# Left-over query units moved to the end of the loop in an attention, expert and router kernel

## The chip, the cores and the metric

The kernel runs on one core of a Trainium2 chip. The core has a matmul engine (TensorE, PE in the profile, with its weight loads shown as PEld), three elementwise engines (VectorE or DVE, ScalarE or ACT, GpSimd or POOL), and SyncE (SP), which issues most of the transfers; each engine takes its instructions in the order in which they were written. The metric is the device time of one execution in microseconds, as the median of several.

## The reference

Three layers stand behind each other, all in float32:

```python
# 1: attention, 4 batches, 8 heads, 576 queries, head size 64: only the 32 largest scores of a row count
scores = scale * np.matmul(q, k.transpose(0, 1, 3, 2))
kth = np.partition(scores, -32, axis=-1)[..., -32:-31]
scores = np.where(scores >= kth, scores, -1e9)
attn = softmax(scores); x = attn @ v            # then 2304 tokens of 512
# 2: a dense layer, 512 -> 2048 -> 512
h = x @ w_in; g = h * np.clip(h + 3.0, 0.0, 6.0) / 6.0; x = g @ w_out
# 3: each token goes to the best of 8 experts (cosine with expert_emb over tau)
expert_idx = argmax(logits)
out[mask] = gate_w * (np.maximum(x[mask] @ w1[e], 0.0) @ w2[e])
```

The largest of a row are found exactly, and the products are taken as sums of rounded high and low parts, so that one float32 product is three matmuls.

## The kernel before

**Units.** Attention is cut into 72 units of 128 score rows by two heads' 576 keys. Of a batch's 576 queries, 512 make four tiles (`t` 0 to 3) by four pairs of heads (`p`): 16 units of kind `"t"`. The 64 queries that are left over of two pairs of heads make one unit of kind `"r"`, two in a batch. `units` lists them in the order in which they run: in each batch the eight of tiles 0 and 1, one `"r"`, four, the other `"r"`, and four.

**Steps.** A loop of 76 steps (`step(i, last)`) runs the units as a pipeline: step i scores unit i, selects the top 32 of unit i-1, masks unit i-2, takes the exponent of unit i-3, turns unit i-4 and, in odd steps, multiplies units i-5 and i-4 with v. A step also takes one **item** of the dense layer: an eighth of the hidden width (two columns of 128) for a group of 256 tokens, 24 matmuls of 256 columns (`s1`, in two halves `s10`, `s11`), the gate on ACT, DVE and POOL (`gate`, `swish`, `large`, `small`), and in the next step the 12 matmuls of 512 columns of that item (`s20`, `s21`). Four strings (FIRST, MID, THEN, ODD) write out by hand in which order a step issues its parts. A step in `PAUSE` takes no item. A group is pushed when its two tiles of tokens are there, so that its eight items come in later steps.

**Norms.** `embed` scales the expert vectors behind steps 4 to 8: a Square, eight tiny matmuls, a Sqrt, whose table has to be loaded on ACT (and that of Exp again after it), and three DVE instructions.

**Weights.** Up to step 19 the steps also split w_in and w_out into a high part, which stays, and a low part, which goes to `lo_dram`. Each item fetches its two low blocks of 512 KB again (`fetch`, L283), one item ahead, on SP, whose instructions wait in line: behind the query, key and value loads, the copies of key halves (`ship`), and the stores.

**Keys.** Batch 0 takes its scores from plain float32 keys. From batch 1 on `prep` splits each pair's keys and queries two steps before they are needed: two copies of 128x576 on ACT (`need_k`), the lows on POOL, and two `ship` transfers.

**After the loop** the items that are left (eight of the last tiles, eight of the left-over tokens, whose columns went to `x_dram` and are read back by `finish_rest`) are recorded by `whole`, the routing of finished groups beside them, and there a scheduler sets the order. `ahead` loads the first expert's weights (`load1`), ids (`load_ids`) and tokens in the same stretch. `last[6]` of the last item and the eight experts follow, once more in written order.

Of the kernel before, what the change touches and what calls it, by code (L numbers as in the profile page):

```python
# [8 lines left out]
F32 = mybir.dt.float32  # L9
# [29 lines left out]
PAUSE = (13, 17, 31, 35, 49, 53, 67, 71)  # L39
# [17 lines left out]
AHEAD = 600  # L57
SIDE = 600


def fused_kernel(tc: tile.TileContext, *args):
# [6 lines left out]
    x_dram = tc.dram_tile([4, 128, CH], F32, name="x_dram")  # L68
# [3 lines left out]
    with ExitStack() as held:  # L72
# [4 lines left out]
        over_ = layers(tc, *args, y_dram, g_dram, x_dram, tbl, lo_dram, flag, pools, consts)  # L77
        rare = nc.values_load(flag[0:1, 1:2], min_val=0, max_val=NT + 1)  # L78
        with tc.If(rare > 0):
            over_()  # L80
            again = nc.values_load(flag[0:1, 0:1], min_val=0, max_val=1)
            with tc.If(again > 0):
                layers(tc, *args, y_dram, g_dram, x_dram, tbl, lo_dram, None, pools, consts)()
# [13 lines left out]
def layers(tc: tile.TileContext, qt, kt, v, w_in, w_out, embt, tau, w1, w2, out, y_dram, g_dram, x_dram, tbl, lo_dram, flag, pools, consts):  # L97
# [39 lines left out]

    def half_a():
        turn[0] ^= 1
        return bank_a[:, turn[0], :]  # L140
# [13 lines left out]
    def embed(part):  # L154
# [6 lines left out]
        elif part == 1:  # L161
            emb["ones"] = mp.tile([128, 128], F32, tag="ug", name="onesf", bufs=1)
# [3 lines left out]
        elif part == 2:  # L166
            onesf, sq = emb["ones"], emb["sq"]
            emb["pe"] = pe = bank_h
# [182 lines left out]
    def need_v(i):  # L351
# [3 lines left out]
        if (b, p) in V:  # L355
            return
        t = vp.tile([128, 5, 128], F32, tag="v", name="vt")
        nc.sync.dma_start(out=t, in_=v[b, p])
        V[b, p] = t
# [60 lines left out]
    def take(i, g):  # L420
        nc.scalar.copy(sbuf[i % NS][:, :, HS * g:HS * g + HS], ps_[i][:, :, :HS])  # L421
# [99 lines left out]
    def finish(i):  # L521
        u = units[i]
        av = avs[i]
        if u[0] == "r":
            _, b, p0 = u
            xq = mp.tile([128, DM], F32, tag="wf", name="xq", bufs=4)[:, :128].rearrange("d (a t) -> d a t", a=2)
            nc.scalar.copy(xq.rearrange("d a t -> d (a t)"), av)
            nc.sync.dma_start(out=x_dram[p0:p0 + 2, :, 64 * b:64 * b + 64].rearrange("n d t -> d n t"), in_=xq)
# [8 lines left out]
    def finish_low(i):  # L537
        u = units[i]
        av = avs.pop(i)
        if u[0] == "r":  # L540
            return
# [6 lines left out]

    def finish_rest():

        X = [xp.tile([128, 4, 256], F32R, tag=n, name=n) for n in ("xh", "xl")]
        for g in range(2):
            c = slice(128 * g, 128 * g + 128)
            raw = mp.tile([128, 4, 128], F32, tag="wf", name="xr", bufs=4)
            nc.sync.dma_start(out=raw, in_=x_dram[:, :, c].rearrange("k d t -> d k t"))
            nc.scalar.copy(X[0][:, :, c], raw)
            nc.vector.tensor_tensor(X[1][:, :, c], raw, X[0][:, :, c].bitcast(F32), op=ALU.subtract)
        push_group(X, [16, 17])

# [10 lines left out]
    def push_group(X, gs):  # L570
# [7 lines left out]
        def s1(q, half=None):  # L578
# [11 lines left out]
            if half != 0:  # L590
                state[q, "h"] = bank_h[:, :2 * nt]
                lows_[0].pop(m0 + q)
                fetch(0, m0 + q + 1)
# [16 lines left out]
        def s2(q, part=None):  # L610
# [16 lines left out]
            if part != 0 or len(gs) == 1:  # L627
                state.pop(q)
                lows_[1].pop(m0 + q)
                fetch(1, m0 + q + 1)  # L630
# [16 lines left out]
    def route(ysb, g):  # L647
        state = {}

        def bank():  # L650
            turn[1] ^= 1
            return bank_t[turn[1]]

# [18 lines left out]
        if g % 4 == 3 and g < 12:  # L672
# [592 lines left out]
```

## Time and profile before

| | us |
|---|---|
| median of 3 runs | 1068.36 (1067.37 to 1068.99) |
| the profiled execution | 1068.97, of which its span 1067.0 |
| PE busy | 967.8 (91%), PEld 838.1 (79%) |
| DVE, ACT, POOL busy | 765.8 (72%), 714.4 (67%), 630.1 (59%) |
| steps 0 to 21 | 0 to 219.1 |
| steps 22 to 71 | 219.1 to 670.7 |
| steps 72 to 75 and the 16 items behind the loop | 670.7 to 809.4 |
| last item's rows, and the experts | 809.4 to 1067.0 |

A busy share is the union of an engine's instructions; a matmul's end is modelled, so that matmuls which wait for their issue look busy. Steps are told apart by L430, the first instruction of `pairs`, which step i issues once for unit i, near the step's end, on DVE. The windows below are cut at the starts of L430: what is called step i runs from unit i-1's L430 to unit i's (units and steps are counted from 0).

### The profile page before, as it was taken

What the parts mean: (1) busy time and instruction counts of PE and PEld (TensorE: products, weight loads), DVE (VectorE), ACT (ScalarE), POOL (GpSimd) and SP (SyncE); (2) the same over time, 40 slices, a digit from 0 to 9 for tenths busy, and PEclk for the clock granted to TensorE, in tenths of its full rate; (3) what the DMA queues carried; (4) which work ended last, traced back from release to release, by engine and by line L of the source; (5) the groups of instructions that cost most, each with busy time, mean ns of one, the idle gap of its engine ahead of it and who ended that gap; (6) DMA issues with size and microseconds to landing.
All of it is one profiled execution on the core that took longest, in us unless ns stands there. A gap on an engine that the chain in (4) does not pass through costs nothing. (4 is left out here: it accounts for less than half of the span.)

```text
span 1067.0 us, 20818 instructions
## 1 busy us (share of the span) xinstructions
PE 967.8 (91%) x7172; PEld 838.1 (79%) x7172; DVE 765.8 (72%) x2344; ACT 714.4 (67%) x1437; POOL 630.1 (59%) x786
## 2 busy tenths in 40 slices
PE   3655797999999999999889999999989999999994
PEld 1333575888988898988789889899978888889993
DVE  6999999898899988899978899611243464445640
ACT  4889899887788887788867788632334444445540
POOL 3678999876678986678876677723231352223310
PEclk9976699899999999999989999999999999999997
DMA  5445676574534664534666443457674465554600
GB/s 182 161 149 166 223 247 217 174 255 136 159 115 127 153 249 139 163 110 133 129 180 193 137 130 116 118 176 192 203 261 168 118 230 199 188 189 173 232 19 21
DMA packets 87665, 176.89 MB, mean 166 GB/s; under 512 B 18941, under 2 KB 34448, under 8 KB 87551
## 3 DMA queue, kind: packets, MB, share of 16 engines
q1 hardware_dynamic: 82975, 165.62, 49.6%
q0 software_dynamic: 4416, 9.80, 2.8%
q8 instruction: 58, 0.95, 0.4%
q14 instruction: 56, 0.46, 0.1%
q10 hardware_dynamic: 160, 0.07, 0.0%
HBM read 152.82 MB, written 19.41 MB: 161 GB/s over the span
## 5 line engine op out<-in xcount | busy, mean ns | idle before, releaser
L467 POOL TENSOR_TENSOR s<-s,z 128x576 f32<-128x576 f32 x144 | 187.6, 1303 | 70.6 <-ACT z L463 69.4
L589 PE MATMUL bank_h<-xh,vh 128*128 128x256 f32 x576 | 173.0, 300 | 1.8 <-DVE u L601 1.7
L589 PE MATMUL bank_h<-xh,lo 128*128 128x256 f32 x576 | 165.5, 287 | 5.3 <-DMA lo<-lo_dram 5.3
L589 PE MATMUL bank_h<-xl,vh 128*128 128x256 f32 x576 | 165.2, 287 | 0.4 <-DVE xl L545 0.4
L449 DVE MAX8 A<-left 128x8 f32<-128x288 f32 (+1 forms) x288 | 159.7, 596 | 0.0
L500 PE MATMUL bank_t<-ident,s 128*128 128x128 f32 x648 | 109.1, 291 | 31.1 <-ACT s L487 15.9
L608 POOL TENSOR_TENSOR gl<-u,gh 128x512 fp32r<-128x512 f32 x72 | 93.2, 1295 | 60.7 <-ACT gh L605 60.7
L421 ACT COPY s<-ps_sc 128x576 f32<-128x576 f32 x144 | 92.5, 643 | 50.3 <-PE ps_sc L414 21.5
L500 PEld LDWEIGHTS bank_t<-ident,s 128*128 128x128 f32 x648 | 80.9, 148 | 54.0 <-ACT s L487 17.5
L505 ACT COPY pt<-bank_t 128x384 f32<-128x384 f32 x216 | 102.5, 478 | 30.8 <-PE bank_t L500 30.8
L624 PE MATMUL y<-wh,gl 128*128 128x512 f32 x288 | 113.6, 400 | 8.7 <-POOL gl L608 8.7
L624 PE MATMUL y<-wh,gh 128*128 128x512 f32 x288 | 117.4, 408 | 0.1
L589 PEld LDWEIGHTS bank_h<-xh,lo 128*128 128x128 f32 x576 | 111.9, 194 | 6.5 <-DMA lo<-lo_dram 6.4
L589 PEld LDWEIGHTS bank_h<-xh,vh 128*128 128x128 f32 x576 | 112.0, 194 | 5.0 <-DVE u L601 3.1
L624 PE MATMUL y<-lo,gh 128*128 128x512 f32 x288 | 114.4, 397 | 0.5 <-DMA lo<-lo_dram 0.5
L473 ACT ACTIVATE s<-s,nb 128x576 f32<-128x576 f32 x144 | 113.1, 787 | 1.7 <-POOL s L467 1.6
L589 PEld LDWEIGHTS bank_h<-xl,vh 128*128 128x128 f32 x576 | 112.1, 195 | 1.1 <-DVE xl L545 0.7
L463 ACT ACTIVATE z<-s,nb 128x576 bf16<-128x576 f32 x144 | 111.2, 779 | 1.1 <-POOL nb L457 1.1
L1007 POOL DMA_INDIRECT out_dram<-ob,idt x21 | 24.4, 1160 | 138.5 <-ACT ob L1004 88.9
L601 DVE SCALAR_TENSOR_TENSOR u<-u,bank_h 128x512 f32<-128x512 f32 x72 | 49.1, 683 | 74.3 <-ACT u L597 71.4
L597 ACT ACTIVATE u<-bank_h,half 128x512 f32<-128x512 f32 x72 | 49.6, 689 | 76.5 <-PE bank_h L589 76.5
L830 DVE TENSOR_TENSOR l<-a,h 128x1024 fp32r<-128x1024 f32 x64 | 77.2, 1242 | 30.8 <-ACT h L829 28.7
(239 smaller groups left out, 2664.7 us busy)
## 6 DMA issues: line engine op xcount, KB each, us to landing
lo<-lo_dram SPq DMA_DIRECT2D x144, 512.0 KB
a<-in_moe_w_dram SPq DMA_DIRECT2D x64, 512.0 KB
w<-in_moe_w_in_dram SPq DMA_DIRECT2D x16, 512.0 KB
lo_dram<-wf SPq DMA_DIRECT2D x32, 256.0 KB
w<-in_moe_w_out_dram SPq DMA_DIRECT2D x16, 512.0 KB
kraw<-in_k_dram SPq DMA_DIRECT2D x48, 144.0 KB
qraw<-in_q_dram SPq DMA_DIRECT2D x48, 128.0 KB
vt<-in_v_dram SPq DMA_DIRECT2D x16, 320.0 KB
```

The costliest lines, as they stand in the source:

```text
L421: nc.scalar.copy(sbuf[i % NS][:, :, HS * g:HS * g + HS], ps_[i][:, :, :HS])
L449: nc.vector.max(A[:, n, 8 * r:8 * r + 8], src[:, n, :w])
L463: nc.scalar.activation(zb_[n], tile_of(i, n), AF.Relu, bias=sel[i][1][:, n, 1:2], scale=-BIG)
L467: nc.gpsimd.tensor_tensor(s, s, zb_[n], op=ALU.subtract)
L473: nc.scalar.activation(s, s, AF.Exp, bias=sel[i][1][:, n, 0:1], scale=SCALE, accum_out=sums[i][:, n:n + 1])
L500: nc.tensor.transpose(pp[:, 128 * k:128 * k + 128], e[:, 128 * (3 * c + k):128 * (3 * c + k) + 128], ident)
L505: nc.scalar.copy(pts[i][:, 3 * c:3 * c + 3, :].rearrange("p k n -> p (k n)"), tb_.pop((i, c))[:, :384])
L589: nc.tensor.matmul(ph[:, a, :], w, x[:, k, :], start=(k == 0 and n == 0), stop=(k == 3 and n == 2))
L597: nc.scalar.activation(u, state[q, "h"], AF.Relu, bias=half, scale=1.0 / 6.0)
L608: nc.gpsimd.tensor_tensor(state[q][1], state.pop((q, "u")).rearrange("p (a n) -> p a n", a=2), state[q][0].bitcast(F32), op=ALU.subtract)
L624: nc.tensor.matmul(state["y"][o], x[:, a, c], w, start=(f == 0 and n == 0), stop=(f == 15 and n == 2))
L830: nc.vector.tensor_tensor(lo, x, hi.bitcast(F32), op=ALU.subtract)
```

## The change

The `"r"` units of all batches stand behind the 64 `"t"` units, those of batch 3 first; their keys are loaded anew into tiles of the pool `kp` (`load_k`) and, but for batch 3, their values too (`rest_v`). `PAUSE` is step 13 alone, so that a group's eight units come in the eight steps in which another's eight items run. The left-over tokens' columns go straight into one group's tiles (`finish`, `finish_low`), and `x_dram` is gone. The Square, matmuls, Sqrt and scaling of `embed` stand behind steps 18 to 21, `setup` behind step 24. `fetch` ahead of time is left out where the weights are not stored yet (`ahead_of`). The first half of unit 0's scores goes to `bank_t`, not to the one score buffer. Nine items stay behind the loop, and those are written out by hand, with `behind(n, k)` placing the routing, the ids, the first expert's weights and tokens between their parts. `choose` and `rank` of groups 12 and 13 come in the loop.

```diff
-PAUSE = (13, 17, 31, 35, 49, 53, 67, 71)
+PAUSE = (13,)
...
+    def ahead_of(n, m):
+        if stored[0] >= min(32, 4 * m + 4):
+            fetch(n, m)
+
     units = []
     for b in range(B):
-        t = [[("t", b, t, p) for p in range(4)] for t in range(4)]
-        r = [("r", b, 0), ("r", b, 2)]
-        units += t[0] + t[1] + r[:1] + t[2] + r[1:] + t[3]
+        units += [("t", b, t, p) for t in range(4) for p in range(4)]
+    for b in (B - 1,) + tuple(range(B - 1)):
+        units += [("r", b, 0), ("r", b, 2)]
...
             for a in range(2):
-                if b < PLAIN:
-                    rest_k[i, a] = kraws[b, p + a]
-                else:
-                    rest_k[i, a] = raw = lp.tile([128, S], F32, tag="kraw", name="kraw", bufs=2)
-                    for n in range(2):
-                        nc.sync.dma_start(out=raw[64 * n:64 * n + 64, :], in_=kt[b * H + 2 * (p + a) + n][64 * n:64 * n + 64, :])
+                rest_k[i, a] = raw = kp.tile([128, S], F32, tag="k", name="krs")
+                for n in range(2):
+                    nc.sync.dma_start(out=raw[64 * n:64 * n + 64, :], in_=kt[b * H + 2 * (p + a) + n][64 * n:64 * n + 64, :])
...
+    def rest_v(i):
+        if i < NU and units[i][0] == "r" and units[i][1] < B - 1:
+            for a in range(2):
+                get_v(units[i][1], units[i][2] + a)
...
+        if i == 0 and g == 0:
+            for n in range(2):
+                d = slice(64 * n, 64 * n + 64)
+                nc.tensor.matmul(bank_t[n][:, :HS], Q[u][d, :], kraws[u[1], u[3]][d, :HS], start=True, stop=True)
+            return
...
-        if g % 4 == 3 and g < 12:
+        if g in (3, 7, 11, 13):
             side.extend((choose, rank))
...
-        if i in (4, 5, 6, 7, 8):
-            embed((4, 5, 6, 7, 8).index(i))
-        if i == 20:
+        if i in (4, 18, 19, 20, 21):
+            embed((4, 18, 19, 20, 21).index(i))
+        if i == 24:
             setup()
...
+        base = len(moe) - 8
+        def behind(n, k):
+            n -= base
+            if (n, k) == (0, 1):
+                place()
+            elif (n, k) == (0, 3):
+                side.popleft()()
...
+            elif (n, k) == (1, 3):
+                side.popleft()()
+                choose()
+            elif (n, k) == (2, 0):
+                rank()
+                place()
...
+            elif (n, k) == (3, 1):
+                expert(0)
+                load1(0)
+            elif (n, k) == (3, 3):
+                load_ids(0, 0, 2)
+            elif (n, k) == (4, 0):
+                for x in bl[0][:2]:
+                    get(0, x)
+            elif (n, k) == (6, 0):
+                turn_in(0, bl[0][0])
...
+            elif (n, k) == (6, 3):
+                load2(0)
+                expert(1)
+            if (n, k) in ((4, 1), (4, 3), (5, 1), (5, 3)):
+                split_1(0, ((4, 1), (4, 3), (5, 1), (5, 3)).index((n, k)))
+
         with tc.manual_schedule():
+            at.close()
+            pools_()
+            for n in range(len(moe)):
+                a = moe[0]
+                part(a, 1, 0)
+                behind(n, 0)
+                part(a, 1, 1)
+                for k in (2, 3, 4, 5):
+                    part(a, k)
+                behind(n, 1)
+                for o in range(2):
+                    last[6](last[0], o)
+                    behind(n, 2 + o)
+                last = moe.popleft()
```

On ACT, the Sqrt of the norms (`nr`) with the two loads of tables stood behind step 7, between the casts of weights (`vh`). Before:

```order
L535 CAST xh<-bank_a 128x128 x2
L173 ACT_TABLE_LOAD
L173 ACTIVATE nr<-bank_h 128x8
L263 CAST vh<-wf 128x2x256
L473 ACT_TABLE_LOAD
```

Now it stands behind step 20, with no weights beside it, between the query's cast (`qh`) and the masks (`z`):

```order
L400 CAST qh<-qraw 128x256
L174 ACT_TABLE_LOAD
L174 ACTIVATE nr<-bank_a 128x8
L480 ACTIVATE z_150<-s_147,nb 128x576
L522 COPY pt<-bank_t_121 128x384
L490 ACT_TABLE_LOAD
```

The two loads moved from a step that splits two blocks of weights to one that splits none.

On ACT in step 17 (`w` are the weights' words, `u` and `gh` an item's gate, `kst` and `qh` the split keys and queries) there was no item before:

```order
L250 ACTIVATE w_1713<-w_1713 128x512
L250 ACTIVATE w_1718<-w_1718 128x512
L263 CAST vh<-wf 128x2x256
L421 COPY s_146<-ps_sc 128x2x288
L505 COPY pt<-bank_t_123 128x384
L463 ACTIVATE z_152<-s_148,nb 128x576
L505 COPY pt<-bank_t_122 128x384
L487 ACTIVATE s_147<-s_147,sums 128x576 x2
L535 CAST xh<-bank_a 128x128
L527 COPY xq<-bank_a 128x128
L421 COPY s_146<-ps_sc 128x2x288
L392 CAST qh<-qraw 128x256
```

and now there is one:

```order
L251 ACTIVATE w_1708<-w_1708 128x512
L251 ACTIVATE w_1715<-w_1715 128x512
L607 ACTIVATE u<-bank_h,half 128x512
L264 CAST vh<-wf 128x2x256
L438 COPY s_145<-ps_sc 128x2x288
L522 COPY pt<-bank_t_122 128x384
L480 ACTIVATE z_151<-s_147,nb 128x576
L522 COPY pt<-bank_t_121 128x384
L504 ACTIVATE s_146<-s_146,sums 128x576 x2
L615 CAST gh<-u 128x512
L552 CAST xh<-bank_a 128x128 x2
L438 COPY s_145<-ps_sc 128x2x288
```

`u` and `gh` came in, and the copy of left-over columns (`xq`) went out.

On SP behind the loop (`a` is the first expert's weights in four transfers, `lo` a low block, `idt` the ids by which the first expert's tokens are gathered) the ids stood ahead of the weights. Before:

```order
L806 TENSOR_LOAD ordi
L806 ISA x2
L811 ISA
L811 DMA idt_9809<-tbl 128x2x2
L816 ISA
L816 DMA a_9811<-in_moe_w_dram 128x1024
```

Now they stand behind the weights' last transfer and a low block:

```order
L808 DMA a_9864<-in_moe_w_dram 128x1024
L284 DMA lo_9881<-lo_dram_61 128x1024
L803 ISA
L803 DMA idt_9863<-tbl 128x2x2
L284 DMA lo_9912<-lo_dram_60 128x1024
```

The ids' transfer moved from ahead of the four to behind them.

## Rows read from the trace of the kernel before

**Rows 1.** Windows by stage: length; PE, PEld, DVE, ACT, POOL busy; clock, DMA, GB/s

```profile
112.90:219.10 106.20, 91.08 (x714) 73.50 (x710) 99.01 (x306) 95.61 (x198) 98.26 (x110) 0.89 0.66 211
219.10:670.70 451.60, 441.80 (x3761) 397.79 (x3760) 406.58 (x1427) 364.84 (x796) 336.46 (x464) 0.99 0.52 153
670.70:809.40 138.70, 132.92 (x907) 118.52 (x905) 40.38 (x96) 53.08 (x98) 49.42 (x55) 0.99 0.63 192
```

**Rows 2.** Windows: eight steps with an item each, one paused step, one long step

```profile
546.90:621.60 74.70, 74.70 (x617) 67.71 (x616) 65.01 (x227) 58.56 (x128) 52.50 (x73) 1.00 0.52 161
...
629.70:637.30 7.60, 7.33 (x98) 5.52 (x97) 7.25 (x27) 7.19 (x16) 6.33 (x9) 1.00 0.58 208
...
531.60:546.90 15.30, 12.49 (x91) 11.51 (x90) 8.07 (x28) 6.96 (x16) 9.04 (x14) 0.78 0.81 221
```

**Rows 3.** Timeline of PE behind the loop: start, duration; first matmuls of two items

```profile
728.32 0.28 PE L589 MATMUL bank_h<-xh,vh 128*128 128x256 f32 x1
...
733.94 0.28 PE L589 MATMUL bank_h<-xh,vh 128*128 128x256 f32 x1
```

**Rows 4.** Waits of PE, 219 to 671: us in total, times, longest one

```profile
PE bank_h L589 <- DMA lo<-lo_dram: 5.3, 3, 2.8
```

**Rows 5.** Timeline of SP's queue at the turn to batch 3

```profile
528.13 1.61 SPq L349 DMA_DIRECT2D kst<-kraw  x2
529.84 0.54 SPq L283 DMA_DIRECT2D lo<-lo_dram  x1
```

**Rows 6.** Timeline of the first step, PE and DVE; in brackets: idle before, releaser

```profile
7.12 1.33 PE L414 MATMUL ps_sc<-kpl,qpl 64*128 64x288 f32 x4 [0.73 <-ACT s L421]
...
9.17 0.47 DVE L430 TENSOR_TENSOR ps_sc<-ps_sc,s 128x288 f32<-128x288 f32 x1 [1.30 <-ACT s L421]
```

**Rows 7.** Windows of steps 8, 9 and 10

```profile
70.20:82.90 12.70, 6.04 (x47) 3.43 (x43) 10.54 (x34) 11.08 (x22) 7.25 (x9) 0.63 0.40 132
82.90:94.00 11.10, 7.92 (x45) 5.61 (x47) 11.00 (x34) 10.03 (x20) 9.13 (x11) 0.50 0.46 148
94.00:103.50 9.50, 4.42 (x33) 2.77 (x29) 9.47 (x34) 8.55 (x20) 8.41 (x10) 0.86 0.51 167
```

**Rows 8.** Timeline of the norms: ACT's table load, DVE's scaling

```profile
72.62 1.28 ACT L173 ACT_TABLE_LOAD   x1
...
85.14 0.86 DVE L176 TENSOR_SCALAR nr<-nr,tb 128x8 f32<-128x8 f32 x1
```

**Rows 9.** Windows of steps 16, 17 and 18

```profile
158.50:168.70 10.20, 8.10 (x45) 5.27 (x43) 10.13 (x32) 10.00 (x20) 10.04 (x9) 1.00 0.84 284
168.70:179.70 11.00, 9.20 (x88) 6.59 (x89) 10.93 (x33) 9.30 (x20) 10.84 (x12) 0.84 0.46 115
179.70:191.60 11.90, 7.50 (x49) 6.80 (x48) 9.68 (x30) 11.35 (x24) 11.21 (x12) 0.84 0.75 247
```

**Rows 10.** L235 on DVE, 0 to 51 and 112.9 to 191.6: busy, mean ns, idle

```profile
L235 DVE TENSOR_SCALAR wf<-w 128x512 int32<-128x512 int32 x7 | 2.8, 419 | 5.8 <-DMA w<-in_moe_w_in_dram 5.8
...
L235 DVE TENSOR_SCALAR wf<-w 128x512 int32<-128x512 int32 x13 | 9.9, 763 | 2.1 <-DMA lo_dram<-wf 2.1
```

**Rows 11.** Waits of PE, 702 to 810

```profile
PE y L624 <- POOL gl L608: 3.5, 2, 3.1
PE pxt L1087 <- ACT ysl L635: 0.7, 1, 0.7
```

**Rows 12.** Timeline behind the loop: order known (DVE), ids and weights (SP), gather (POOL)

```profile
779.11 0.16 DVE L771 CAST ordi<-res 1x8 int32<-1x8 f32 x1
...
782.44 0.41 SPq L811 DMA_DIRECT2D idt<-tbl  x1
783.06 2.30 SPq L816 DMA_DIRECT2D a<-in_moe_w_dram  x4
...
785.36 0.99 POOL L845 DMA_INDIRECT xg<-y_dram,idt  x1 [7.53 <-DMA idt<-tbl]
```

**Rows 13.** Window of the burst of weights behind the loop

```profile
785.00:790.00 5.00, 1.94 (x7) 1.23 (x6) 1.83 (x2) 2.68 (x3) 3.22 (x3) 0.86 0.99 390
```

More of the change, by code (lines that the diff above doesn't have):

```diff
@@ L136, in layers, with bank @@
     turn = [0, 0]
+    def bank():
+        turn[1] ^= 1
+        return bank_t[turn[1]]
     def half_a():
@@ L420, in take @@
     def take(i, g):
+        if i == 0 and g == 0:
+            for n in range(2):
+                nc.scalar.copy(sbuf[0][:, n, :HS], bank_t[n][:, :HS])
+            return
         nc.scalar.copy(sbuf[i % NS][:, :, HS * g:HS * g + HS], ps_[i][:, :, :HS])
@@ L525, in finish @@
             _, b, p0 = u
-            xq = mp.tile([128, DM], F32, tag="wf", name="xq", bufs=4)[:, :128].rearrange("d (a t) -> d a t", a=2)
-            nc.scalar.copy(xq.rearrange("d a t -> d (a t)"), av)
-            nc.sync.dma_start(out=x_dram[p0:p0 + 2, :, 64 * b:64 * b + 64].rearrange("n d t -> d n t"), in_=xq)
+            if "r" not in xt:
+                xt["r"] = [xp.tile([128, 4, 256], F32R, tag=n, name=n) for n in ("xh", "xl")]
+            nc.scalar.copy(xt["r"][0][:, p0:p0 + 2, 64 * b:64 * b + 64], av.rearrange("d (a t) -> d a t", a=2))
             return
@@ L547, in finish_low @@
             push_group(xt[b, t // 2], [4 * b + t - 1, 4 * b + t])
[L549 to L558, printed above, removed]
     moe = deque()
@@ L592, in s1 @@
                 lows_[0].pop(m0 + q)
-                fetch(0, m0 + q + 1)
+                ahead_of(0, m0 + q + 1)
         def gate(q):
@@ L629, in s2 @@
                 lows_[1].pop(m0 + q)
-                fetch(1, m0 + q + 1)
+                ahead_of(1, m0 + q + 1)
         def out_y(o):
@@ L724, in place @@
             tc.add_to_no_dep_group("places", w_.ins)
-    def whole(item, last):
-        if item:
-            q, s1, gate, swish, large, small = item[:6]
-            s1(q)
-            with tc.high_priority(offset=AHEAD):
-                gate(q)
-                swish(q)
-                large(q)
-                small(q)
-        if last:
-            last[6](last[0])
-        return item
     def part(item, k, *half):
@@ L830, in split, with pools_ @@
         nc.vector.tensor_tensor(lo, x, hi.bitcast(F32), op=ALU.subtract)
-    def split1(r):
-        a1 = ws1[r]
-        h1, l1 = [late["w1"].tile([128, 4, F2], F32R, tag=t, name=t) for t in ("h1", "l1")]
-        for k in range(4):
-            split(h1[:, k, :], l1[:, k, :], a1[:, k, :])
-        ws1[r] = (h1, l1)
-    def tokens(r, bl, pps, tk=None):
-        if r not in tok:
-            tok[r] = [(tk if TURNS.index(r) % 2 else late["tk"]).tile([128, 4, CAPS[TURNS.index(r) % 2]], F32R, tag=t, name=t) for t in ("xh_", "xl_")]
-        xh_, xl_ = tok[r]
-        for n, o, m in bl:
-            xg = late["xg"].tile([128, DM], F32, tag="xg", name="xg")
-            nc.gpsimd.indirect_dma_start(out=xg[:m, :], out_offset=None, in_=y_dram,
-                                         in_offset=bass.IndirectOffsetOnAxis(ap=idts[r][:m, n, 0:1], axis=0))
-            pp = pps()
-            for k in range(4):
-                nc.tensor.transpose(pp[:, k, :m], xg[:m, 128 * k:128 * k + 128], ident[:m, :m])
-            nc.scalar.copy(xh_[:, :, o:o + m], pp[:, :, :m])
-            nc.vector.tensor_tensor(xl_[:, :, o:o + m], pp[:, :, :m], xh_[:, :, o:o + m].bitcast(F32), op=ALU.subtract)
-    def ahead():
+    def pools_():
         def pool(key, **kw):
@@ L935, in layers @@
         looping[0] = False
-        rest = True
-        while moe or side:
-            if not rest and "order" in late and "w1" not in late:
-                at.close()
-                ahead()
-            for _ in range(2):
-                if side:
-                    with tc.high_priority(offset=SIDE):
-                        side.popleft()()
-                with tc.high_priority(offset=SIDE):
-                    if chosen[0] < scored[0] and scored[0] % 2 == 0:
-                        choose()
-                        rank()
-                    while spots:
-                        place()
-            last = whole(moe.popleft() if moe else None, last)
-            if rest and len(moe) <= 1:
-                rest = False
-                finish_rest()
-        assert "w1" in late and done_groups[0] == NG - 2
         hs, xg_, gg_, xt_ = {}, {}, {}, {}
```

52 lines of the change are left out of this document (28 added, 24 removed).

## The prediction

> **What bounds the kernel now.** I read the windows by stage first. From step 22 on PE is busy in 441.8 of 451.6 us, and behind the loop in 132.9 of 138.7, while DVE falls from 406.6 of 451.6 to 40.4 of 138.7 [rows 1]. So from step 22 to the end of the items the time is PE's, and the question is what PE does not do there. In the steps 12 to 21 no engine is full: PE is busy 91.1 of 106.2 us at a granted clock of 0.89 (a mixture of 2.4 and 1.2 GHz), DVE 99.0, POOL 98.3, ACT 95.6 [rows 1]. There it is the three elementwise engines, with the weights to split, that set the length of a step.
>
> Then I read single steps. Eight steps with an item each take 74.7 us, 9.34 a step, with PE busy all the time and its weight loads busy for 67.7, which is 91% [rows 2]. A paused step takes 7.6, with weight loads busy for 5.52, which is 73%, and DVE for 7.25, which is 95% [rows 2]: it is bound by DVE, although PE looks busy for 7.33. An item behind the loop costs 733.94 - 728.32 = 5.62 us of PE [rows 3]. The same item makes a step only 9.34 - 7.6 = 1.74 us longer, since a step without one has PE waiting; the steps around a pause run a little ahead, so that not all of the difference comes back.
>
> Last I read the waits. From 219 to 671 the longest of PE are for low blocks, 5.3 us in three waits [rows 4]. They stand at the turns of batches, where SP copies split keys first and issues the low block behind them [rows 5]. The step with the longest of them takes 15.3 us, 6.0 more than an item step, and its clock is 0.78, so some of it ran at 1.2 GHz after PE had stood [rows 2]. Without the wait of 2.8 that leaves 3.2 for the clock; waits and clock make 8.5. Behind the loop PE waits 3.5 + 0.7 = 4.2 us [rows 11], the most for POOL, whose `gl` stood behind two gathers that wait for the ids [rows 12].
>
> **The change part by part.** The sum is made against the profiled execution, 1068.97 (span 1067.0 and 1.97 around it), which is 0.6 above the median.
>
> *First step.* PE's second half of unit 0 waits 0.73 us until ACT has emptied the one score buffer, and DVE starts 1.30 late behind it [rows 6]. With the other buffer PE need not wait, but ACT still has three copies to make. Between 0 and -1.3 I take the middle, -0.65.
>
> *Norms out of the steps 4 to 8.* Step 10, which has the same two blocks of weights and no norms, takes 9.5 us; steps 8 and 9 take 12.7 and 11.1 [rows 7]: 3.2 + 1.6 = 4.8 saved. DVE is full in steps 9 and 10, so it is a real saving; it would be less only if the weights' transfers were late next, which rows 7 don't show (DMA share 0.40 to 0.51). Value -4.8, at the least -3.5.
>
> *Norms behind steps 18 to 21.* What left comes back: two table loads of 1.28 on ACT and the scaling on DVE, of which L176 alone was 0.86 [rows 8]. In an item step ACT is busy 58.56 / 8 = 7.3 of 9.34 us and DVE 65.0 / 8 = 8.1 [rows 2], so they have 2.0 and 1.2 us free, and PE hides that much. The tiny matmuls have to wait for a half of `bank_a`. Between 0 and the 4.8 that it cost before I take 2.4.
> The page "ScalarE: Activation LUTs" of the Trainium skill (section What ACT_TABLE_LOAD costs) gives each switch 1283 ns for the load and some 1380 more for a drain. The trace agrees with the load, 1.28 [rows 8], and not with the drain: two such switches would be 5.3, and step 8, which has both, is only 3.2 longer than step 10 [rows 7]. By the page the term would be 2.8 higher and the time 1053.
>
> *Steps 12 to 21.* Batch 1 now starts with unit 16 and no longer 18, so its four preps (two copies on ACT, two lows on POOL each) move from steps 16 to 19 into 14 to 17, and step 17 gets an item. Step 16 has all of that, weights, a prep and an item, and takes 10.2; step 17, without the item, 11.0; step 18, with an item, a prep and one block of weights instead of two, 11.9, of which DVE stood 2.1 for a store [rows 9, 10]. The mean of the ten steps is 10.6 [rows 1]. If 14 to 17 take 11.4 each, near the longest of them, this costs 4 x 0.8 = 3.2. Steps 18 to 21 keep an item each and lose their preps; I give nothing for that, since with an item each PE needs its 9.34 there as well. Bounds: all four like step 16, -1.6, and all four 2.1 over the mean, +8.4. For this one more item is done before step 22: that gain lies in the count below.
> DVE's L235 takes 419 ns in the first steps and 763 on the mean in these [rows 10]. The page "SBUF — State Buffer" of the Trainium skill (section SBUF: two separate sides) says why: DVE and GpSimd share a pair of ports as an exclusive lock, and the loser blocks for the other's whole instruction. By that rule every low that moves into steps 14 to 17 can hold up DVE, which is full there, and the term would lie at its upper bound of 8.4 and not at 3.2, which makes 1055; the trace agrees with the stretching, but the steps that already had preps are no longer for it than 10.2 to 11.9.
>
> *Steps 22 to 71.* There were 50 steps, six of them paused, in 451.6 us. Now all 50 carry an item: 50 x 9.34 = 467.0, if nothing waits. The left-over units cost PE what the others do within some tenths, and their keys and values are loaded two steps ahead. There are two turns of batches in this stretch, as before; the eight left-over units, with their values queued on SP behind PE's products, come to it. Waits between 0 and 11, where 8.5 stood before [rows 2, 4]: I take 4.5, since the steps are longer now and POOL has more room in them, so that `ship` holds SP up for less. Together 471.5 - 451.6 = +19.9.
>
> *Behind unit 71.* Before, four items of the loop and 16 behind it stood in the 138.7 us after 670.7; now there are four and nine. PE was full there [rows 1], so seven items are worth 7 x 5.62 = 39.3 [rows 3]: -39.3. (The other six of them are in the steps 22 to 71, the seventh in step 17.)
>
> *Waits behind the loop.* What PE waited for the gathers' queue, 3.5, is moved, not removed. `rank` now stands between the halves of the first product of the fourth of the nine items, and the order of the experts is known some 4 us behind it (estimate: a dozen DVE instructions like L771 with their spacing, and one held up). Before, the ids were issued 3.2 after L771 and the weights 0.6 later [rows 12]. Now SP issues the weights at 3.2, then a low block, then the ids: 2.6 MB. At the 390 GB/s of that burst [rows 13] they take 6.7 us, with 2 until the first arrives 11.9 after the order is known, so 15.9 after the rank. PE comes to that low block after 1.4 + 2 x (2.8 + 2.8) + 0.2 = 12.8 us (a product of an item is half of 5.62) and waits 3.1. The gathers (2.3) and POOL's `gl` (1.3) are then done at 19.5, before PE needs them at 21.8. The rank's own matmul waits for `choose`: take 1. The last rows' copy, 0.7, stays. Together 4.8 for 4.2: +0.6. Bounds: no wait but the last, -3.5; at the stage's mean of 192 GB/s [rows 1] the 2.6 MB take 13.6, +7.
>
> *Experts.* The stretch from 809.4 has the same instructions and the same releasers: 0.
>
> Sum: -0.65 - 4.8 + 2.4 + 3.2 + 19.9 - 39.3 + 0.6 = -18.65, so 1050.3 for the profiled execution and, with the 0.6, about 1050 for the median.
>
> **The rivals.** *The waits for low blocks come back in full.* SP's line is the same, ships ahead of low blocks at each turn, and with no pause before a turn there is no step in which a fetch could get ahead. For it: rows 5. Against it: 3.2 of the 8.5 is a clock that fell once. Waits of 11 and not 4.5, and 2.5 more behind the loop: 1050 + 9 = 1059.
>
> *An item costs in a step what it costs behind the loop.* If PE's time is the whole price, six more items make the steps 6 x 5.62 = 33.7 longer, and not 19.9: 1064. For it: PE is busy in 98% of the stretch. Against it: the weight loads of a paused step, 73% against 91% [rows 2].
>
> *All covers hold.* No wait in the loop (-4.5), norms hidden (-2.4), steps 14 to 17 as long as the mean (-3.2): 1050 - 10 = 1040. For it: the eight item steps without a gap of PE [rows 2]; against it: three covers have to hold at once.
>
> *Slower: no pause, no recovery.* An item step has DVE 8.1 of 9.34 us busy, and ACT, DVE, POOL and PE wait for each other through one score buffer. If without pauses each delay is handed on from step to step, the 50 steps take more than 9.34. From 9.34 + (18.65 + 4.5) / 50 = 9.80 on, with no other wait, the change gains nothing; at 9.9 the time is 1050.3 - 4.5 + 28, some 1074. For it: the longest stretch that rows show without a pause is the one of eight steps [rows 2]. Against it: in those eight PE has no gap at all.
>
> **How the numbers follow.** The forecast, 1050, has a chance of 0.55, with a range of its own from 1044 to 1057 (its terms' bounds drawn together, since they are independent). Waits in full, 1059: 0.15. Item at full price, 1064: 0.07. All covers hold, 1040: 0.14. Slower, above 1070: 0.08. That nothing of it shows, 0.01. The range from 1040 to 1063 holds the forecast's 0.55, the 0.15, and half or more of the two beside it, about 0.8. A measurement can tell 0.2% of this kernel, 2.1 us, from no change: faster than 1066.2 has 0.55 + 0.15 + 0.14 and nearly all of the 0.07 less some for their spread, 0.88; within 0.2% 0.04; slower 0.08.
>
> **What would show it.** Windows cut at the steps' `pairs`: steps 8 and 9 near 9.5 us; 14 to 17 between 10 and 12; step 71's `pairs` near 691 and no step from 22 on under 8; the loop's last stretch and nine items about 100 us long, with PE's waits there near 5 us, the longest for `lo` and not for `gl`. Wrong it would be with a mean item step above 9.6, with waits for low blocks above 8 us in the loop, with steps 14 to 21 more than 8 us longer together, or with PE standing over 8 us between the nine items.

## The result, and the profile after

The changed kernel takes 1055.46 us (median of 4 runs, 1052.04 to 1056.70) where the kernel before takes 1068.20 (4 runs, 1067.37 to 1068.99): ratio 0.9876, 95% interval 0.9851 to 0.9900 (estimated from all runs, so it is not quite the quotient of the medians). The forecast was 1050, its range 1040 to 1063. The gain is 12.7 us; the sum had 18.65. The profiled executions differ by nearly as much as the medians, 1053.9 of span against 1067.0, so the missing 5.5 us can be looked for in the trace.

First the windows of the changed kernel, cut at the same events as before: to unit 11's `pairs`, to unit 21's, to unit 71's, to the first transpose of `ysl`, to the end. The columns are the length, then busy us (and count) of PE, PEld, DVE, ACT and POOL, the granted clock, the DMA share and GB/s. The second to fourth line answer to [rows 1].

```profile
0.00:109.60 109.60, 60.65 (x310) 36.98 (x312) 100.08 (x330) 83.65 (x164) 76.81 (x91) 0.84 0.54 176
109.60:226.00 116.40, 96.01 (x704) 79.53 (x701) 102.66 (x306) 99.41 (x202) 100.12 (x108) 0.92 0.64 204
226.00:698.20 472.20, 470.87 (x3954) 423.04 (x3954) 410.83 (x1446) 374.77 (x812) 347.88 (x482) 1.00 0.55 163
698.20:796.90 98.70, 94.30 (x738) 84.17 (x736) 28.91 (x84) 40.68 (x80) 36.73 (x41) 1.00 0.67 218
796.90:1053.90 257.00, 239.94 (x1473) 210.89 (x1473) 117.75 (x188) 114.81 (x182) 68.79 (x66) 0.98 0.45 153
```

Set against the kernel before, stage by stage, with what the prediction gave:

| stage | before | after | difference | forecast |
|---|---|---|---|---|
| to unit 11 | 112.9 | 109.6 | -3.3 | -0.65 - 4.8 = -5.45 |
| steps 12 to 21 | 106.2 | 116.4 | +10.2 | +3.2 + 2.4 = +5.6 |
| steps 22 to 71 | 451.6 | 472.2 | +20.6 | +19.9 |
| behind unit 71 | 138.7 | 98.7 | -40.0 | -39.3 + 0.6 = -38.7 |
| experts | 257.6 | 257.0 | -0.6 | 0 |

The two large terms came out. Of the 5.5 us that are missing, 4.6 stand in the steps 12 to 21, where no large term was. Single steps of the changed kernel: 8 and 9 (they answer to [rows 7]), then 15 to 22 (16 to 18 answer to [rows 9]).

```profile
71.10:80.80 9.70, 4.14 (x39) 2.66 (x35) 9.67 (x34) 9.56 (x21) 8.60 (x10) 0.99 0.52 168
80.80:90.20 9.40, 7.29 (x41) 4.74 (x43) 9.37 (x31) 8.44 (x18) 8.15 (x10) 0.54 0.55 179
...
143.80:155.70 11.90, 9.92 (x84) 7.33 (x84) 11.83 (x35) 11.90 (x26) 11.74 (x13) 1.00 0.63 183
155.70:168.10 12.40, 9.66 (x62) 8.24 (x60) 11.78 (x32) 12.20 (x25) 12.23 (x12) 0.95 0.80 257
168.10:181.20 13.10, 12.52 (x102) 10.97 (x101) 12.32 (x34) 11.93 (x25) 12.94 (x14) 0.92 0.85 269
181.20:192.20 11.00, 8.25 (x54) 6.96 (x53) 10.10 (x31) 10.02 (x22) 10.84 (x12) 1.00 0.67 213
192.20:202.10 9.90, 8.19 (x75) 6.69 (x73) 8.36 (x30) 6.96 (x17) 9.74 (x15) 1.00 0.63 187
202.10:216.90 14.80, 12.45 (x71) 11.72 (x72) 7.94 (x28) 6.82 (x15) 5.83 (x8) 0.77 0.53 195
216.90:226.00 9.10, 7.53 (x76) 6.65 (x75) 8.02 (x27) 8.88 (x17) 5.31 (x10) 1.00 0.01 2
226.00:236.10 10.10, 10.10 (x66) 8.96 (x66) 9.31 (x33) 9.06 (x21) 6.74 (x11) 1.00 0.71 246
```

Steps 8 and 9 are 3.0 and 1.7 shorter, as said. Steps 16 and 17 are up 2 us each, with DVE, ACT and POOL full. The odd one is step 20, 202.1 to 216.9: 14.8 us with DVE, ACT and POOL half idle and a clock of 0.77, so part of it ran at 1.2 GHz. PE's waits say what ended last, first in step 20, then in the loop [rows 4], then behind it [rows 11]:

```profile
PE bank_h L599 <- DMA lo<-lo_dram: 2.3, 1, 2.3
...
PE bank_a L535 <- ACT pt L522: 0.9, 3, 0.3
PE bank_t L517 <- ACT pt L522: 0.3, 1, 0.3
...
PE y L634 <- DMA lo<-lo_dram: 3.4, 2, 2.4
PE pxt L1084 <- ACT ysl L645: 0.7, 1, 0.7
PE bank_a L748 <- DVE pos L711: 0.3, 1, 0.3
```

In step 20 PE stood 2.3 us for a low block. In the loop's 472 us, where 4.5 was forecast for low blocks, it waited for none. Behind the loop the longest wait is for `lo` and no longer for `gl`. What follows the wait of step 20 shows in the starts of the matmuls of 256 columns:

```profile
205.55 0.58 PE L599 MATMUL bank_h<-xh,lo 128*128 128x256 f32 x1 [2.35 <-DMA lo<-lo_dram]
...
206.36 0.41 PE L599 MATMUL bank_h<-xh,lo 128*128 128x256 f32 x1
206.58 0.41 PE L599 MATMUL bank_h<-xh,vh 128*128 128x256 f32 x1
...
211.27 0.29 PE L599 MATMUL bank_h<-xl,vh 128*128 128x256 f32 x1
211.39 0.28 PE L599 MATMUL bank_h<-xh,lo 128*128 128x256 f32 x1
```

They follow each other after some 0.21 us up to 211.27 and after 0.12 from there on. The 5.7 us from 205.55 to 211.27, at half speed, lose 2.9.

### The profile page after: what moved, and what is told of

Same layout as the page of the kernel before. It is cut to its first block, busy times and chain, and to the rows that moved or that the text cites. A ratio compares the mean times of both kernels' runs of the same rounds, so it can differ in the third digit from the quotient of the medians.

```text
span 1053.9 us, 20817 instructions
## 1 busy us (share of the span) xinstructions
PE 961.8 (91%) x7172; PEld 834.6 (79%) x7172; DVE 760.2 (72%) x2350; ACT 713.3 (68%) x1436; POOL 630.3 (60%) x786
## 5 line engine op out<-in xcount | busy, mean ns | idle before, releaser
L517 PE MATMUL bank_t<-ident,s 128*128 128x128 f32 x648 | 107.3, 289 | 24.3 <-ACT s L504 16.2
L535 PE MATMUL bank_a<-pt,vt 128*64 128x128 f32 (+1 forms) x1600 | 95.9, 278 | 4.5 <-ACT pt L522 4.5
L535 PEld LDWEIGHTS bank_a<-pt,vt 128*64 128x64 f32 x1600 | 85.8, 145 | 15.1 <-issue 9.1
```

The costliest lines, as they stand in the source:

```text
L517: nc.tensor.transpose(pp[:, 128 * k:128 * k + 128], e[:, 128 * (3 * c + k):128 * (3 * c + k) + 128], ident)
L535: nc.tensor.matmul(av[64 * n:64 * n + 64, c0:c1], vt[:, k, 64 * n:64 * n + 64], pt[:, k + 5 * n if k < 4 else 4, c0:c1], start=(o == 0), s ...
```

## The experiments

Beside the runs below the kernel before took 1070.4 to 1070.6 (medians; single runs from 1065.6 to 1074.5). Ratios are to the runs of the kernel before beside each, and on those the kernels are compared.

**The late block of step 20 (a_fetch).** `ahead_of` leaves a low block out where its weights are not all stored yet. In step 19 that holds for one block, the eighth of the first group: the last store comes a few instructions later, and the block is asked for only in step 20's own product.

```
         stored[0] += 1
+        if n == 31:
+            fetch(0, 7)
```

> The changed kernel with the low block of the eighth item fetched right behind the last store of split weights (step 19), and not inside the product that needs it (step 20). Late-fetch theory: the 14.8 us of step 20 are a step of about 10 with a wait of 2.3 for the block and some 2.4 that TensorE lost at half clock behind it; both go, step 20 takes 9.5 to 10.5, the time falls by 4 to 5 us to about 1051. Rival, elementwise bound: the step is long because of what was moved into it (norms, preps of the next batch), then it stays above 13 and the time within 1 us. Rival, queue: the fetch now stands behind the store on the queue and comes only some 1 us before it is needed or later; a wait of about 1 stays and the clock falls all the same: 1 to 2 us gained.

Measured: 1053.94 (1052.23 to 1055.11), ratio 0.9844, interval 0.9819 to 0.9868. Step 20 in its profile, the stage 12 to 21, and the stretch behind the loop:

```profile
202.20:211.80 9.60, 9.60 (x72) 9.09 (x72) 7.96 (x28) 6.82 (x15) 5.80 (x9) 1.00 0.86 305
...
109.50:220.90 111.40, 92.99 (x704) 76.20 (x701) 102.14 (x307) 99.28 (x202) 100.13 (x108) 0.94 0.68 214
693.60:794.80 101.20, 95.63 (x737) 85.22 (x735) 28.80 (x83) 40.56 (x80) 36.55 (x41) 0.98 0.67 212
```

The step takes 9.6 and not 14.8, at full clock, and the stage 111.4, 5.0 less. The queue shows how little was amiss: SP asked for the block at 198.35, behind another low block and a load of values, and now asks at 197.48, ahead of both. A wait of 2.3 cost 5.2, the rest being the 2.9 of half clock behind it. So the late-fetch theory holds for the step, and both rivals fall. Against the changed kernel's first runs the whole time fell by less than the 4 to 5 us expected, 3.4 by the ratios, whose intervals overlap (against a_again below it is 5.0): the stretch behind the loop (last line) took 101.2 in this execution, where it had taken 98.7.

**The same kernel again (a_again).**

> The changed kernel as it is, once more, as the measure for the runs beside it and for how far its executions differ. If the long step 20 (14.8 us, wait for a low block and half clock) and the waits of 3 to 6 us between the nine items are a race of transfers against TensorE, they differ from profile to profile: step 20 between 9.5 and 15, the waits for low blocks behind the loop between 3 and 6.5, everything from step 22 to 71 within 1 us of 472. If they are fixed, step 20 takes 14 to 15 again.

Measured: 1059.31 (1056.24 to 1061.17), ratio 0.9891 (0.9865 to 0.9917), so the gain is 11 to 13 us in both sets of runs. Step 20, the loop, and the stretch behind it:

```profile
202.30:216.40 14.10, 12.22 (x71) 11.49 (x71) 7.93 (x27) 6.80 (x15) 5.76 (x8) 0.76 0.58 203
225.50:698.40 472.90, 471.16 (x3955) 423.10 (x3955) 410.90 (x1447) 374.68 (x812) 347.01 (x482) 1.00 0.55 163
698.40:800.80 102.40, 95.85 (x737) 85.22 (x735) 28.83 (x83) 40.56 (x80) 37.39 (x41) 0.98 0.65 210
```

The loop repeats to 0.7 us, step 20 comes late again, and the stretch behind the loop took 102.4, not 98.7: the waits for low blocks there were 5.6 us in this execution, and the clock fell once. The 98.7 was the luckiest that was seen of this code (101.2 in a_fetch, 102.2 in a_norms and 103.5 in a_nolow, which change nothing there).

**The norms (a_norms).** `if i in (4, 5, 6, 7, 8)` again, with the tiles that `embed` had before.

> The changed kernel with the norms back in steps 4 to 8. Theory: steps 8 and 9 become 4.7 longer again, and the steps 19 to 22 give back what the norms cost there, 1 to 2.4 us; the time rises by 2.3 to 3.7 to about 1058. Rival, norms are as dear behind step 18 as in the front (4.8, with a drain at each table load): the time stays within 0.5. Rival, norms cost the clock there: the fall to half clock in step 20 goes with them and the time falls by 2 or more.

Measured: 1060.76 (1056.88 to 1062.71), ratio 0.9902 (0.9876 to 0.9928), 2.8 us over the changed kernel's 0.9876 and 1.2 over a_again's; the intervals overlap, so the windows have to price it. Steps 8 and 9, then 21 and 22:

```profile
70.40:83.60 13.20, 6.64 (x39) 4.09 (x37) 10.46 (x34) 11.27 (x22) 7.39 (x9) 0.63 0.40 130
83.60:94.70 11.10, 7.92 (x45) 5.61 (x47) 11.00 (x33) 10.03 (x20) 9.13 (x11) 0.50 0.49 149
...
221.40:229.20 7.80, 7.76 (x78) 7.04 (x77) 7.76 (x28) 6.70 (x14) 4.92 (x7) 1.00 0.01 2
229.20:238.80 9.60, 9.60 (x64) 8.58 (x63) 8.26 (x30) 8.60 (x22) 8.05 (x13) 1.00 0.75 265
```

In front they cost 5.2 here (24.3 against 19.1), behind step 20 1.8 (9.1 + 10.1 against 7.8 + 9.6). Step 20 was late in this run too (13.7 us, clock 0.75), so the norms were not what made it late.

**The ids behind the low block (a_ids).** `load_ids` at (4, 1) instead of (3, 3), `get` at (4, 2) instead of (4, 0).

> The changed kernel with the first expert's ids asked for half an item later, behind the next low block on SP and not ahead of it. SP theory: the waits for low blocks between the nine items (2.4 + 1.0 us) stand because SP itself stands 5.5 us for the scattered rows to land before it may issue the ids, with the low block behind; ahead of the ids the block comes in time, the waits fall below 0.8, the gathers come when they came, the time falls by 2.5 to 3.4 us to about 1052.5. Rival, burst (the prediction's reason): the 2 MB of weights ahead of the block make it late whatever the order, waits of 2 and more stay and the time is the same within 1. Rival, gathers: they become late with the ids, gl stands behind them on POOL and TensorE waits 2 to 3 for it: same or slower.

Measured: 1056.92 (1052.45 to 1059.93), ratio 0.9867 (0.9839 to 0.9895): the same. PE's waits behind the loop:

```profile
PE y L634 <- DMA lo<-lo_dram: 6.2, 2, 3.8
```

The block was asked for while SP did not stand, and still came 10.9 us later. The SP theory falls. This profile also showed step 20 at 9.5 us at full clock, though nothing there was changed: its steps 18 and 19 took 12.2 and 11.2, 2.5 more than in the changed kernel's, and PE came to the block after it had landed. It is a race that a slower step can win.

**The weights in four pieces (a_spread).** With the edit of a_fetch, `load1(0)` asks for one quarter at each of (3, 1), (3, 3), (4, 1) and (4, 3), so one low block stands between two quarters; the ids as in a_ids.

> The changed kernel with three edits: the low block of the eighth item fetched behind the last store, the first expert's 2 MB of weights asked for in four pieces, one behind each low block, instead of all ahead of one, and the ids half an item later. Burst theory: the low block waited for between the nine items came 9.5 to 11 us after it was asked for, because 2 MB stood ahead of it; with 0.5 MB ahead it needs about 5, the waits behind the loop fall from 3.4 to 6.5 to under 1, and their clock stays at 2.4 GHz: the stretch behind the loop takes 95 to 97 (98.6 to 103 now), and with the step 20 mended the time is 4 to 8 us under the changed kernel's. Rival, scatter: the queue is held up by the scatter of the rows (4 KB packets take 1 to 4 us behind it, instead of 0.16), then a low block still needs 7 and more and 2 to 4 us of waits stay. Rival, split: the pieces come too late for ACT and DVE to split and the first expert starts late: no gain.

Measured: 1050.58 (1049.74 to 1050.65), ratio 0.9814 (0.9790 to 0.9839), 8.7 us under a_again on the same chip, and its five runs lie within 0.9 us, those of a_again within 5. Its stretch behind the loop, and the waits in it:

```profile
694.30:791.60 97.30, 94.33 (x738) 84.12 (x736) 29.11 (x84) 40.66 (x80) 36.62 (x41) 1.00 0.68 221
```

```profile
PE y L636 <- DMA lo<-lo_dram: 2.0, 2, 1.5
```

Against a_again 5.1 us came from behind the loop and 4.6 from step 20 (9.5 for 14.1). The waits are 2.0, not under 1 as expected, for 5.6 in a_again. So the burst was a cause. (The ids are moved here as well, but that alone changed nothing in a_ids.) Of the 2.0 us left, 1.5 belong to the last low block, which stands behind the second weights.

**Without the last scatters (a_noscatter).** `spots.popleft()` for `place()` in `behind`, which leaves out the four scatters of rows there.

> The changed kernel without the four scatters of rows behind the loop (those of the last groups' tokens are left out, so these tokens reach no expert; all else stays). Scatter theory: the slow packets of 4 KB right behind the scatters go, the low block asked for behind the weights comes after 6 to 7 us and not 9.5 to 11, TensorE waits under 1 us for it and the stretch behind the loop takes 95 to 97: 2.5 to 5 us less. Burst theory: the slow packets belong to the burst itself; the block comes after 9 and more, the wait of 2 to 4 stays and the time is the same within 1.

Measured: 1052.19, ratio 0.9822 (0.9793 to 0.9850), but in two groups (1050.53 to 1052.52, and 1057.28 and 1058.32); the profiled one is of the upper group. The waits of PE in this run, then SP's issue of the first expert's weights and the GB/s of 752 to 772 in slices of 0.5 us, first of a_again, then of this run:

```profile
PE y L634 <- DMA lo<-lo_dram: 3.1, 2, 1.8
```

```profile
759.91 2.15 SPq L808 DMA_DIRECT2D a<-in_moe_w_dram  x4
GB/s 393 336 197 98 320 139 426 410 51 0 0 0 0 51 106 90 123 16 49 33 8 90 147 246 229 328 418 426 443 377 378 402 443 418 401 385 352 207 157 238
```

```profile
759.47 1.98 SPq L808 DMA_DIRECT2D a<-in_moe_w_dram  x4
GB/s 418 459 180 180 131 401 401 49 0 0 0 0 0 131 131 410 361 131 90 319 352 385 352 377 418 410 418 426 418 418 401 322 329 394 393 385 353 328 442 336
```

With the scatters the DMA engines move less than 150 GB/s from 758.5 to 763.5, though SP asks for a low block at 757.95 and for the 2 MB of weights from 759.91 on; they pass 300 again at 764.5, 4.6 us after the first of the weights were asked for. Without the scatters the block that was asked for at 757.55 brings 410 at 759.5, and the weights bring 300 and more from 761.5 on, 2.0 us after they were asked for. The wait for the block behind the burst fell from 3.9 to 1.3 (the 1.8 is the last block's, at 792.9); it was 2.4 in the changed kernel's own profile. The block still came 8.8 us after it was asked for (9.5 to 11 with the scatters), between what the two theories said. So both have a share, the scatters some 1 to 2.6 us of the wait, and these are single executions: the stretch behind the loop took 98.4, no less than the 98.7 of the luckiest one with scatters. Why some of these runs are 6 us faster than the profiled one was not seen; its step 20 was late (14.3 us), which may have been spared to the others.

**One pause more (a_17).** The edit of a_fetch, and `PAUSE = (13, 17)`; `behind` takes the tenth item.

> The changed kernel with the low block of the eighth item fetched early and a pause in step 17 as well, so that one item less is done in the loop and ten stand behind it. The item behind the loop costs 5.6. Cheap-item theory (the prediction's): the item made steps 15 to 18 hardly longer, they give back 0 to 1 and the time is 4 to 5.6 above that of the early fetch with one pause. Rival, dear item: the item lengthened steps that ACT, DVE and POOL already filled by what it costs them, 2 to 4 us of the 4.8 by which steps 15 to 17 grew; the time is 1.5 to 3.5 above it. Rival, full price: the time is the same.

Measured: 1058.67 (1056.22 to 1061.71), ratio 0.9891 (0.9859 to 0.9924), 0.0047 or 5 us over a_fetch. The stages 12 to 21, 22 to 71 and behind:

```profile
109.50:221.50 112.00, 91.91 (x670) 75.09 (x667) 101.97 (x306) 98.20 (x200) 98.85 (x107) 0.88 0.69 214
221.50:690.30 468.80, 468.10 (x3947) 421.95 (x3946) 418.07 (x1445) 372.74 (x808) 346.37 (x482) 1.00 0.54 161
690.30:800.30 110.00, 103.72 (x782) 92.36 (x780) 29.72 (x84) 43.57 (x85) 38.33 (x43) 0.97 0.66 207
```

With an item less the steps 12 to 21 are not shorter, 112.0 for a_fetch's 111.4: step 17 takes 13.0 without its item (13.1 with it), POOL busy for 12.8. In that stage the item was free, and what made 16 and 17 longer is something else. (The clock was lower in step 17, 0.65, but PE, busy for 10.8 of the 13.0, was not what was late.) The loop fell by 3.9 and the rest rose by 8.8 (its clock 0.97). The loop has 50 items in both, but each comes one step later here; why it is shorter so was not followed. So the total of 5 is as the cheap-item theory said, its parts are not.

**The split of the keys (a_nolow).** In `lows`, the subtraction is passed over for the four key tiles of batch 1 (their low parts are left out).

> The changed kernel with the four subtractions of POOL that split the keys of batch 1 left out (those keys' low parts are not formed), in the steps where its preps now stand. With them steps 15, 16 and 17 take 11.8, 12.5 and 13.1 us, and DVE is busy 11.8 to 12.3 in them, where step 14 takes 10.0. Port theory: POOL's instructions hold up DVE's, so that DVE's busy time falls by 1 us or more a step along with POOL's 1.3, and steps 15 to 18 become 3 to 5 us shorter together. Rival, ACT: ACT's two more copies set the length (it is busy 11.8 to 12.3 as well), DVE's busy time falls and idles instead, and the steps stay within 1 us.

Measured: 1050.40 (1049.53 to 1054.77), ratio 0.9828 (0.9796 to 0.9860). DVE's bit operation on the weights' words in the steps 16 to 19, first with the subtractions (the changed kernel), then without; behind the count stand busy us and mean ns:

```profile
L243 DVE SCALAR_TENSOR_TENSOR wf<-w,wf 128x512 int32<-128x512 int32 x5 | 7.5, 1507 | 0.1
```

```profile
L243 DVE SCALAR_TENSOR_TENSOR wf<-w,wf 128x512 int32<-128x512 int32 x5 | 3.6, 710 | 0.1
```

The same five instructions take 0.8 us less each, and the steps 15 to 19 fall from 58.3 to 53.3 together (11.7, 10.9, 11.7, 10.2, 8.8). Step 20's wait is 0.6 there. So ACT's copies alone do not set these steps, and POOL's subtractions do. How is not settled. DVE's words wait for them, as the port theory says: DVE is busy 3.6 us less in these steps. But DVE's other instruction on words (L236) takes 811 ns for 652, and POOL itself was full in the steps 15 to 17 (busy 36.9 of 37.4 us) and has 6.5 us less to do in 15 to 19. That it was POOL's own time was not tested apart.

The same instruction in the steps 15 to 19 of the kernel before and of the changed one, with ns at least, in the middle and at most, shows what the new place of the preps did:

```profile
L242 DVE SCALAR_TENSOR_TENSOR wf<-w,wf x7: 693/733/1803, 150.8 to 185.5; 128x512 int32<-128x512 int32 x7
```

```profile
L243 DVE SCALAR_TENSOR_TENSOR wf<-w,wf x7: 1010/1787/1802, 146.7 to 184.9; 128x512 int32<-128x512 int32 x7
```

Before, the four subtractions of the keys ran in the steps 17 to 20, where three of the seven were left to do, and one of the seven took 1.8 us. Now they run in 15 to 18, one in each, and four of the seven take 1.8; together the seven take 10.3 us for 6.4.

**The pauses alone, in the kernel before (b_pauses).** `PAUSE = (13, 17)` and nothing else.

> The kernel before with the pauses in steps 13 and 17 alone, so that six more items are done in the loop; order of the units, norms and the code behind the loop stay as before. Pause theory: the 50 steps from 22 take 50 x 9.36 + 8.5 of waits and clock = 476.5 (before 451.6, +25), the items behind the loop are six fewer, 6 x 5.62 = -33.7: together -8.8, 1059.5. Rival, order theory: with left-over units between the batches the turns are worse without a pause, waits for low blocks and half clocks of 5 us more: 1064. Rival, full price: steps longer by 5.62 for each item, no gain, 1068.

Measured: 1077.12 (1072.96 to 1078.66), ratio 1.0057 (1.0039 to 1.0075): slower, outside all three. The steps 22 to 71 and the stretch behind, then the count of L601 (one for each item) in the loop before and here:

```profile
219.70:685.50 465.80, 451.43 (x3819) 405.80 (x3818) 409.47 (x1429) 367.44 (x797) 337.65 (x467) 0.99 0.52 153
685.50:818.00 132.50, 126.16 (x849) 111.49 (x847) 39.46 (x93) 51.42 (x97) 47.91 (x52) 0.97 0.62 189
```

```profile
L601 DVE SCALAR_TENSOR_TENSOR u<-u,bank_h x44: 668/687/689, 226.7 to 661.5; 128x512 f32<-128x512 f32 x44
```

```profile
L601 DVE SCALAR_TENSOR_TENSOR u<-u,bank_h x46: 661/686/690, 227.3 to 681.5; 128x512 f32<-128x512 f32 x46
```

(Count, then ns at least, in the middle and at most, the first and the last start.) Six pauses fewer, and only two more items done. The queue of items runs empty: a group of eight items is ready eight or ten units after the last one, since left-over units stand between them, so that 18 units have 16 items. The steps 38, 39, 56 and 57 find nothing to take, two in a row each time (step 56: PE busy 6.1 of 11.3 us, clock 0.82), and the last two groups still stand behind the loop: from step 72 on 18 items are left, for 20 before, so two of the last four steps are empty too and the loop does no item more in all. The pauses of the kernel before only spread such empty steps. PE's waits for low blocks in the steps 22 to 71 were only 0.5 us, so the turns that the order theory named are not what made it slower; where the 14.2 us of these steps came from was not followed further.

**Both mended (a_last).** a_spread, with `load2(0)` at (7, 3) and not at (6, 3).

> The kernel with the early fetch and the weights of the first expert in four pieces, and now also the second weights of that expert asked for behind the last low block and not ahead of it. What waits are left behind the loop there are 0.5 and 1.5 us, the longer one for the last low block, which SP could ask for only after it had stood 2.6 us for room for the weights. Theory: the 1.5 goes, the stretch behind the loop falls from 97.3 to about 95.8, the time by 1 to 1.5 to about 1049. Rival: the second weights come late for the first expert and TensorE or the split waits there for as much: the same time.

Measured: 1049.40 (1048.08 to 1051.27), ratio 0.9807 (0.9782 to 0.9831). No wait for a low block is left behind the loop, and its stretch is

```profile
693.60:789.40 95.80, 94.23 (x738) 84.18 (x736) 29.15 (x84) 40.72 (x80) 37.41 (x41) 1.00 0.68 225
```

1.5 less than a_spread's, as expected. The times of the two can't be told apart. Both beat the two kernels of this study, by the ratios: a_last by some 20 us the one before and by 7 to 9 the changed one (its two sets of runs).

## Why the prediction was right, and where it was not

*Direction and size.* Right: faster by 12.7, within the range. The two terms that carry it, +19.9 for 50 steps with an item and -39.3 for seven items, measured +20.6 and, with the waits, -40.0 (forecast with them -38.7). The -40.0 is in part luck: with a_again's 102.4 it is -36.3.

*Steps 12 to 21: the step that failed.* The prediction said that "Steps 18 to 21 keep an item each and lose their preps; I give nothing for that". Low blocks were counted only from step 22 on. But the change lets one fetch out in step 19, and step 20 paid 5.2 for it (a_fetch). Without that, +10.2 would be +5.0 for a forecast of +5.6, and the sum -18.3 for -18.65. The other misses nearly cancel: the front +2.2 and the loop +0.7, against -1.3 behind it, -0.6 in the experts and the -0.6 here. One sign that the prediction had named for being wrong did come: the steps 14 to 21 are 10.6 us longer together (133.8 to 226.0 for 137.5 to 219.1), and the bound was 8. Without the 5.2 of the late block it would be 5.4.

*The preps, +3.2.* Measured +2.8 to the end of step 19 (202.1 for 202.6, from 109.6 for 112.9): 15, 16 and 17 are longer by 5.2 together, 18 and 19 shorter by 2.1. The size is right, in part by luck, "14 to 17 take 11.4 each" is not: they take 10.0 to 13.1. Step 14 has no subtraction of the preps, it is as long as before; they run in 15 to 18. Nor did the step 16 from which the lower bound was taken, and which was to have "all of that", have one before: the first started at 171.1, in step 17. That a step's item costs nothing in this stage is shown (a_17), and that POOL's subtractions do is shown too (a_nolow). The rule of the Trainium skill in "SBUF — State Buffer", section SBUF: two separate sides, that DVE and GpSimd block each other, agrees in kind: 1507 for 710 ns. The prediction's estimate by it, 8.4, was too high: the words took 3.9 us more than before in the steps 15 to 19 (10.3 for 6.4, under a_nolow), and the step that has only one block of weights, 18, did not grow.

*The norms.* -4.8 in front: -4.7 in steps 8 and 9. +2.4 behind: 1.8 (a_norms), less than their two loads of a table, 1.28 each. On ACT the Sqrt follows its load at once:

```profile
217.19 1.28 ACT L174 ACT_TABLE_LOAD   x1
218.48 0.18 ACT L174 ACTIVATE nr<-bank_a 128x8 f32<-128x8 f32 x1
```

By "ScalarE: Activation LUTs" of the Trainium skill, section What ACT_TABLE_LOAD costs, with a drain at each load, the estimate was 5.2; the trace shows the load and no drain behind it.

*First step, -0.65.* +0.2: unit 1's `pairs` starts at 17.57 for 17.35. PE's wait of [rows 6] is gone, but ACT's third copy, and DVE's first work on words, stand behind weights that landed at 7.8 us in this execution, 6.7 before. In the other profiles with this first step unit 1 starts between 17.4 and 18.7: no gain there. Steps 6, 10 and 11 are 1.1 longer together; step 6 with a clock that fell in another place. This was not tried further.

*The loop.* Right in sum, by luck, not in its parts. Of the 4.5 for waits nothing came; instead the eight steps of the left-over units take 9.78 each and the others 9.38 (78.2 / 8 and 394.0 / 42), for a forecast of 9.34 for all. The reason for -39.3 was half told: it took the seven items as freed by the pauses, but b_pauses shows that without the new order of units there are no items to do in those steps. (The new order with the old pauses was not run.)

*Waits behind the loop, +0.6.* 2.4 for `lo` at the place named, where 3.1 was forecast, 1.0 for a later block that was not, and 4.4 in all, for 4.8. In other executions the waits for `lo` alone are 4.5 to 6.2 (a_fetch, a_again, a_ids), so the term is rather too small. That 2.6 MB stand ahead of the block was a right reason (a_spread) but not all of it: scatters just ahead slowed the queue (a_noscatter).

*Rivals.* Waits for low blocks did not come back in the loop; an item did not cost its full price; the slower case did not come, the steps stay at 9.4 without any pause. Of the three covers one held, the loop without a wait for low blocks, and its steps were longer by as much.

## What to carry to other kernels

Where work is moved into a loop, count how many pieces are there to take at each step, before the price of one: a pause may only stand where the queue would be empty. When a prefetch gets a condition, list the one step in which the condition fails, and price it with the clock's fall and not only with the wait. A large load belongs in pieces between the small ones that the next product needs.

## What was not expected of the hardware

- A wait of 2.3 us of TensorE cost 5.2, since the matmuls behind it ran at 1.2 GHz for 5.7 us (step 20: clock 0.77 for 14.8 us, 1.00 for 9.6).
- Behind scatters of rows the DMA engines passed 300 GB/s only 4.6 us after 2 MB began to be asked for (a_again); without the scatters it took them 2.0 us (a_noscatter; one execution of each).
- One DVE instruction on 128x512 int32 took 1507 ns on the mean beside POOL's subtractions and 710 without four of them (five instructions each).
